# Tile 0 enters K and Q unscaled, loads are reordered, and GT runs one tile behind, in a linear-attention and SwiGLU block on one Trainium2 core

## The chip, the cores and the metric

The kernel runs on one core of one Trainium2 chip. The metric is the device time of one execution in microseconds (us), as the median of several runs. The core has five engines that run their own instruction queues and meet at semaphores: TensorE (PE in the profile; PEld is its weight load), VectorE (DVE), ScalarE (ACT), GpSimd (POOL) and SyncE (SP). SP computes nothing; here it issues most DMAs. ScalarE's queue issues some of the first ones too.

## The reference

The input x has 2048 rows of 512 numbers in bfloat16. Both branches read the same normalized rows; the result is their sum with x.

```python
def _layernorm(x, axis=-1, eps=1e-5):
    m = jnp.mean(x, axis=axis, keepdims=True)
    v = jnp.var(x, axis=axis, keepdims=True)
    return (x - m) / jnp.sqrt(v + eps)

def _A_ref(x, wqkv, wo):              # B, S, D = 1, 2048, 512
    H = 32; Dh = D // H
    q, k, v = ...                     # x @ wqkv, split into 32 heads of 16
    phi = lambda t: jnp.where(t > 0, t + 1, jnp.exp(t)) + 1e-6
    pq, pk = phi(q), phi(k)
    kv = jnp.einsum("bhsd,bhse->bhde", pk, v)
    z = jnp.einsum("bhsd->bhd", pk)
    num = jnp.einsum("bhqd,bhde->bhqe", pq, kv)
    den = jnp.einsum("bhqd,bhd->bhq", pq, z)[..., None] + 1e-6
    o = num / den
    return (...) @ wo                 # heads side by side again

def _B_ref(x, w_gate, w_up, w_down):  # F = 1792
    g = _silu(x @ w_gate)
    u = x @ w_up
    return (g * u) @ w_down

xn = _layernorm(x)
return x + _A_ref(xn, A_wqkv, A_wo) + _B_ref(xn, B_w_gate, B_w_up, B_w_down)
```

## The kernel before

The 2048 rows are 16 tiles of 128 rows. Every engine's instructions are written in an order chosen by hand: the helper class `_Prog` keeps a list for each engine and, from the keys that an operation reads and writes (`r=`, `w=`), works out the semaphore waits. It does not reorder. A DMA is entered in the list of the engine that issues it, so an engine's queue also holds up the DMAs that stand behind a wait.

The work has two phases. In the first, each tile t goes through these steps, named after the functions in the code:

- `stat(t)`: mean and variance on VectorE (`bns`, `agg`); then `rstd_pow`, which adds epsilon (L297) and raises to the power -0.5 on GpSimd (L304). For tile 0 the add is on VectorE, for the others on GpSimd.
- `xn`: (x - mean) * rstd on VectorE (L286; in halves for tile 0, L329).
- the transpose of xn into `xnT`: on TensorE with a copy by ScalarE for tiles 0 to 3 (`transpose_half`, `transpose_pe`, L313, L320), and by a DMA that SP issues for tiles 4 to 15 (`transpose_dma`, L357).
- `kproj`, `qproj`: four matmuls each into a PSUM bank, K to bank 2(t mod 2), Q to the next one (L366; for tile 0 `proj_half`, L379).
- `exp_k`, `exp_q` on ScalarE: the exponential of K and of Q, and a copy of Q (L402, L408, L412).
- `feat_k` on VectorE: clip the exponential (L419), then max(K, 0) plus it (L428). This gives phi(K), called pk.
- `zsum` on GpSimd adds up pk (L449, L453).
- `gtacc(t)`: GT, the product of xn and pk summed over all tiles in banks 4 to 7 (L461). It stands for kv: the weights of V are multiplied in afterwards.

In the loop, GT runs two tiles behind the projections: tile t's K and Q, then GT of tile t - 2. Before tile 0 is there, TensorE runs matmuls on constants (`fill`, L250) into bank 3.

The second phase is the feed-forward network, 56 steps j of one gate product and one up product (`ffn`, L567), with the finish of the attention, the down products and the output tiles put in between (L739, L750).

The first loads are issued on two queues. SP: x tile 0, x 2, the second half of K's weights, x 3, the last quarter of Q's weights, x 4, and then, after a wait for Q's weights, x 6 to 9, 10 to 11, 12 to 15. ScalarE: x 1, the first half of K's weights, half of Q's, a quarter of Q's, x 5. DMA transposes of the tiles come after all of them on SP. At t = 9 SP issues the gate and up weights in eight pieces of 448 KB each (`wpiece`, L212), then V's weights and WO; after the first z transposes, the down weights in one DMA (L209).

Of the kernel before, what the change touches and what calls it, by code (L numbers as in the profile page):

```python
# [108 lines left out]
def bass_parallel_sum__linear_attn_block__swiglu_ffn__prompt_kernel(  # L109
# [16 lines left out]
    with contextlib.ExitStack() as es:  # L126
        E = es.enter_context

        def sb(name, shape, d=bf):
            return E(nc.sbuf_tensor(name, [P] + shape, d))  # L130

        x_sb = sb("x_sb", [NT, D])
        xn_sb = sb("xn_sb", [NT, D])
        xnT = sb("xnT", [NDC, S])
        wqkv_sb = sb("wqkv_sb", [NDC, 3 * D])
        wo_sb = sb("wo_sb", [NG, D])
# [55 lines left out]
        def xload(eng, h, t0, n, after=()):  # L192
            K.dma(
                eng, lambda: h.dma_start(x_sb[:, t0:t0 + n, :], xv[:, t0:t0 + n, :]),  # L194
                r=list(after), w=[("x", t0 + i) for i in range(n)],
            )

        def wqkv_load(eng, h, name, i, c0, n):
            K.dma(
                eng,  # L200
                lambda: h.dma_start(  # L201
                    wqkv_sb[:, c0:c0 + n, i * D:(i + 1) * D],
                    A_wqkv[c0 * P:(c0 + n) * P, i * D:(i + 1) * D].rearrange("(c p) f -> p c f", p=P),
                ),
                w=[(name, c0)],
            )
# [4 lines left out]
        def wpiece(name, dst, src, c):  # L211
            K.dma("sp", lambda: sp.dma_start(dst[:, c, :], src[c * P:(c + 1) * P, :]), w=[(name, c)])  # L212
# [70 lines left out]
        def xn_dve(t):  # L283
# [52 lines left out]
        def transpose_half(t, b, h):  # L336
            tb = banks[b].bitcast(bf)[:, 0:HD].rearrange("p (c s) -> p c s", c=2)
            K.op(
                "pe",
                [  # L340
                    (lambda c=c: pe.transpose(
                        tb[:, c, :], xn_sb[:, t, (2 * h + c) * P:(2 * h + c + 1) * P], ident[:, :],
                    ))
                    for c in range(2)
                ],
                r=[("xnh", t, h), ("ident",)], w=[bk(b)],
            )
# [14 lines left out]
        def proj(t, b, lo, wname):  # L362
            K.op(
                "pe",
                [
                    (lambda c=c: pe.matmul(  # L366
                        banks[b], xnT[:, c, t * P:(t + 1) * P], wqkv_sb[:, c, lo:lo + D],
                        start=(c == 0), stop=(c == NDC - 1),
                    ))
                    for c in range(NDC)  # L370
                ],
                r=[("xnT", t), (wname, 0), (wname, 2)] + ([(wname, 3)] if wname == "wq" else []), w=[bk(b)],
            )

        def proj_half(t, b, lo, wname, h):
            K.op(
                "pe",
                [
                    (lambda c=c: pe.matmul(  # L379
                        banks[b], xnT[:, c, t * P:(t + 1) * P], wqkv_sb[:, c, lo:lo + D],  # L380
                        start=(c == 0), stop=(c == NDC - 1),
                    ))
                    for c in (2 * h, 2 * h + 1)
                ],
                r=[("xnTh", t, h), (wname, 2 * h)] + ([(wname, 3)] if wname == "wq" and h else []), w=[bk(b)],
            )

        def kb(t):
# [36 lines left out]
        def maxadd(dst, src, e, r, w):  # L425
# [54 lines left out]
        stat(0)  # L480
        stat(1)
        xn_half(0, 0)
        xn_half(0, 1)
# [6 lines left out]
        stat(4)  # L490

        fill(8, 512)
        fill(6, P, [("mv", 0)])
        fill(4, P, [("rstd", 0)])
        transpose_half(0, 4, 0)
        transpose_half(0, 5, 1)
        fill(4, P)
        proj_half(0, kb(0), D, "wk", 0)
        proj_half(0, kb(0), D, "wk", 1)
        transpose_pe(1, 6)  # L500
        exp_k(0)
        proj_half(0, qb(0), 0, "wq", 0)
        proj_half(0, qb(0), 0, "wq", 1)
        exp_q(0)
        kproj(1)
        transpose_pe(2, 7)
# [3 lines left out]
        feat_k(0)  # L510
        xn(3)
        xn(4)
        stat(5)
        kproj(2)
        transpose_pe(3, 4)
# [5 lines left out]
        stat(6)
        feat_k(2)
        gtacc(0)

        STAT = {2: (7,), 3: (8,), 4: (9, 10), 5: (11,), 6: (12,), 7: (13,), 8: (14, 15)}
        XN = {2: (6,), 3: (7,), 4: (8,), 5: (9, 10), 6: (11,), 7: (12,), 8: (13,), 9: (14, 15)}

        for t in range(2, NT):
            if t >= 3:
                kproj(t)  # L530
                exp_k(t)
                qproj(t)
                exp_q(t)
                feat_k(t)
# [4 lines left out]
            if t == 9:  # L539
                for c in range(NDC):  # L540
                    wpiece("wg", wg_sb, B_w_gate, c)
                for c in range(NDC):
                    wpiece("wu", wu_sb, B_w_up, c)
# [18 lines left out]
        def ffn_mm(j, w_sb, wname, b):  # L562
# [283 lines left out]
```

## Time and profile before

| | us |
|---|---|
| median of 3 runs (213.23 to 213.66) | 213.25 |
| the profiled execution, its own time | 213.49 |
| span of the instructions in it | 212.3 |
| DMA transposes of xn tiles: median from issue to landing, 12 of them | 2.5 |
| x, single tiles on SP: median to landing, 4 of them | 4.3 |
| gate weights, 448 KB pieces: median to landing, 4 of them | 5.5 |
| up weights, 448 KB pieces: median to landing, 4 of them | 9.0 |

The span runs from the first instruction to the last one; the run's own time also holds what lies around it. All times in a timeline are counted from the start of the span. A row of a timeline has the start, the duration, the engine, the line of the kernel, the operation, the output and its inputs, the shape, how many instructions are merged in the row, and in brackets how long the engine sat idle before and what ended that. The duration of a merged row of matmuls reaches to the end of the last one, which is still in the array when the next row starts; what a group costs the engine is read from start to start. The granted clock of TensorE was 1.00 over the whole span.

The page's row of DMA load in 40 equal slices shows when the queues are full; the second row is what was moved:

```profile
DMA  5782333897752011110101021102011010110201
GB/s 174 252 216 53 55 70 74 281 388 241 208 173 53 0 25 25 49 27 26 35 16 49 6 31 40 49 0 49 3 49 25 25 25 28 42 33 28 51 28 49
```

A slice is 5.3 us. The first three hold the loads of x and of K's and Q's weights, slices 8 to 12 the weights of the feed-forward network.

### The profile page before, as it was taken

How to read it: one execution, taken by the hardware profiler on the slowest of the kernel's cores; microseconds unless marked ns; L12 is line 12 of the kernel's file. 1: busy time of each engine (PE TensorE's matmuls, PEld its weight loads, DVE VectorE, ACT ScalarE, POOL GpSimd, SP SyncE). 2: the span in 40 equal slices, each digit the busy share in tenths (PEclk: the TensorE clock that was granted, in tenths of full speed). 3: DMA queues.
4: the chain of work that ended last, by engine and by line, in shares of the span. 5: the costliest groups of instructions: out<-in, count | busy, mean ns of one | idle time of the engine just before them, and what ended most of it. 6: DMA issues, size and time to landing. Idle time of an engine off the chain costs nothing.

```text
span 212.3 us, 2770 instructions
## 1 busy us (share of the span) xinstructions
PE 207.1 (98%) x985; PEld 96.2 (45%) x1004; DVE 119.2 (56%) x240; ACT 68.0 (32%) x118; POOL 72.7 (34%) x95
## 2 busy tenths in 40 slices
PE   7999999999999999999999999999999999999996
PEld 2444444444544444444444444444444444444454
DVE  3799997333554876546373746464656535374121
ACT  2686666666353332213122302112032213121000
POOL 2548886648021544032130442121414031221100
DMA  5782333897752011110101021102011010110201
GB/s 174 252 216 53 55 70 74 281 388 241 208 173 53 0 25 25 49 27 26 35 16 49 6 31 40 49 0 49 3 49 25 25 25 28 42 33 28 51 28 49
DMA packets 26287, 16.19 MB, mean 76 GB/s; under 512 B 18080, under 2 KB 24864, under 8 KB 26272
## 3 DMA queue, kind: packets, MB, share of 16 engines
q1 hardware_dynamic: 25296, 15.08, 25.8%
q10 hardware_dynamic: 976, 0.92, 1.4%
q8 instruction: 8, 0.13, 0.3%
q14 instruction: 7, 0.06, 0.1%
HBM read 9.70 MB, written 2.10 MB: 56 GB/s over the span
## 4 chain that ended last, share of the span: by engine, by line
PE 94%; DMA 3%; SPq 1%; issue 1%; DVE 1%
PE psum L567 45%; PE psum L750 23%; PE psum L366 12%; PE psum L739 6%; PE psum L461 6%; DMA wqkv_sb<-in_A_wqkv_dram 3%; SPq L194 1%; PE psum L665 0%; PE psum L688 0%; DVE pkq L428 0%; PE psum L379 0%; SPq L201 0%; DVE out_sb L763 0%; DVE ek L419 0%; PE psum L313 0%
## 5 line engine op out<-in xcount | busy, mean ns | idle before, releaser
L582 ACT ACTIVATE sg<-psum 128x512 bf16<-128x512 f32 x56 | 33.4, 598 | 106.9 <-PE psum L567 105.0
L567 PE MATMUL psum<-xnT,wu_sb 128*128 128x512 bf16 x222 | 57.4, 379 | 0.1
L567 PE MATMUL psum<-xnT,wg_sb 128*128 128x512 bf16 x217 | 56.0, 379 | 0.4
L697 POOL TENSOR_TENSOR prod<-pkq,zb 128x512 f32<-128x512 bf16 x16 | 18.6, 1162 | 56.0 <-DVE pkq L428 56.0
L567 PEld LDWEIGHTS psum<-xnT,wu_sb 128*128 128x128 bf16 x224 | 21.9, 98 | 26.5 <-ACT gt_sb L597 0.4
L567 PEld LDWEIGHTS psum<-xnT,wg_sb 128*128 128x128 bf16 x224 | 21.9, 98 | 26.2
L763 DVE TENSOR_TENSOR out_sb<-psum,x_sb 128x512 bf16<-128x512 f32 (+1 forms) x17 | 11.2, 660 | 36.1 <-PE psum L750 36.1
L721 POOL TENSOR_TENSOR pqn<-pkq,rden 128x512 bf16<-128x512 bf16 x16 | 16.9, 1057 | 36.6 <-DVE rden L715 36.6
L588 DVE TENSOR_TENSOR pkq<-psum,sg 128x512 bf16<-128x512 f32 x28 | 19.1, 686 | 18.2 <-PE psum L567 13.6
L366 PE MATMUL psum<-wqkv_sb,xnT 128*128 128x512 bf16 x118 | 28.4, 379 | 0.4 <-DVE pkq L428 0.3
L588 DVE TENSOR_TENSOR xn_sb<-psum,sg 128x512 bf16<-128x512 f32 x28 | 18.8, 671 | 14.2 <-PE psum L567 13.6
L750 PE MATMUL psum<-wd_sb,xn_sb 128*128 128x512 bf16 (+1 forms) x124 | 25.6, 355 | 0.1
L750 PE MATMUL psum<-wd_sb,pkq 128*128 128x512 bf16 x110 | 25.4, 379 | 0.1
L453 POOL TENSOR_TENSOR zacc<-zacc,pkq 128x512 f32<-128x512 f32 x15 | 17.3, 1156 | 7.0 <-DVE ek L419 6.8
L366 PEld LDWEIGHTS psum<-wqkv_sb,xnT 128*128 128x128 bf16 x120 | 11.6, 98 | 14.1 <-ACT xnT L320 0.6
L750 PEld LDWEIGHTS psum<-wd_sb,xn_sb 128*128 128x128 bf16 x126 | 12.3, 98 | 11.9
L750 PEld LDWEIGHTS psum<-wd_sb,pkq 128*128 128x128 bf16 x112 | 11.0, 98 | 13.2
L739 PE MATMUL psum<-m_sb,eq 128*128 128x512 bf16 (+1 forms) x66 | 16.2, 366 | 0.1
L461 PE MATMUL psum<-pkq,xn_sb 128*128 128x512 bf16 x62 | 15.8, 379 | 0.1
L705 DVE TENSOR_REDUCE den<-prod 128x32 f32<-128x512 f32 x16 | 10.9, 684 | 5.9 <-POOL prod L697 5.9
L278 DVE BATCH_NORM_STATS2 stats<-x_sb 128x6 f32<-128x512 bf16 x16 | 10.9, 683 | 4.4 <-DMA x_sb<-in_A_x_dram 4.4
L402 ACT ACTIVATE ek<-psum 128x512 bf16<-128x512 f32 x16 | 9.5, 596 | 8.9 <-DVE pkq L428 3.5
(56 smaller groups left out, 130.6 us busy)
## 6 DMA issues: line engine op xcount, KB each, us to landing
out_dram<-out_sb SPq DMA_DIRECT2D x15, 128.0 KB, 1.7
wg_sb<-in_B_w_gate_dram SPq DMA_DIRECT2D x4, 448.0 KB, 5.5
wu_sb<-in_B_w_up_dram SPq DMA_DIRECT2D x4, 448.0 KB, 9.0
wd_sb<-in_B_w_down_dram SPq DMA_DIRECT2D x1, 1792.0 KB, 7.9
x_sb<-in_A_x_dram SPq DMA_DIRECT2D x2, 512.0 KB, 4.4
x_sb<-in_A_x_dram SPq DMA_DIRECT2D x4, 128.0 KB, 4.3
wqkv_sb<-in_A_wqkv_dram ACTq DMA_DIRECT2D x2, 256.0 KB, 5.2
wqkv_sb<-in_A_wqkv_dram SPq DMA_DIRECT2D x1, 512.0 KB, 10.5
```

Source lines behind the costliest of these rows:

```text
L278: K.op("dve", lambda: dve.bn_stats(stats[:, t, :], x_sb[:, t, :]), r=[("x", t)], w=[("st", t)])
L366: (lambda c=c: pe.matmul(banks[b], xnT[:, c, t * P:(t + 1) * P], wqkv_sb[:, c, lo:lo + D], start=(c == 0), stop=(c == NDC - 1),))
L453: lambda: pool.tensor_tensor(out=zacc[:, :], in0=zacc[:, :], in1=pk, op=ALU.add),
L461: (lambda c=c: pe.matmul(banks[4 + c], xn_sb[:, t, c * P:(c + 1) * P], pkq[:, t, 0, :], start=(t == 0), stop=(t == NT - 1),))
L567: (lambda c=c: pe.matmul(banks[b], w_sb[:, c, fc * P:(fc + 1) * P], xnT[:, c, C * 512:(C + 1) * 512], start=(c == 0), stop=(c == NDC - 1),))
L582: lambda: act.activation(sg[:, j % NSG, :], banks[gb], ACT.Silu),
L588: lambda: dve.tensor_tensor(out=hT(C, fc), in0=banks[ub], in1=sg[:, j % NSG, :], op=ALU.mult,),
L697: lambda: pool.tensor_tensor(out=p, in0=pkq[:, t, 1, :], in1=zb[:, :], op=ALU.mult),
L721: lambda: pool.tensor_tensor(out=pqn[:, t % NPN, :].rearrange("p (h e) -> p h e", e=DH), in0=pkq[:, t, 1, :].rearrange("p (h e) -> p h e", ...
L739: (lambda g=g: pe.matmul(dst, pqnT(t)[:, g, :], m_sb[:, g, lo:hi], start=(g == 0), stop=False,))
L750: (lambda fc=fc: pe.matmul(dst, hT(C, fc)[:, jj * P:(jj + 1) * P], wd_sb[:, fc, lo:hi], start=False, stop=(fc == NFC - 1),))
L763: lambda: dve.tensor_tensor(out=o, in0=src, in1=x_sb[:, t, lo:hi], op=ALU.add),
```

## The change

Tile 0's x is only centred (`xc_half`: x minus mean, no rstd), transposed into a tile of its own, `xcT`, and multiplied by K's and Q's weights; ScalarE multiplies by rstd when it reads the banks (`first_ek`, `first_pk`, `first_eq`, `first_pq`). Tile 0's max(K, 0) is written to SBUF by ScalarE (`kpos`), and VectorE adds it to the clipped exponential (`first_feat`). The normalized tile 0 is still made, whole, for GT, and its `xnT` comes by a DMA transpose at t = 10.

The loads are issued in another order: SP has x 0, x 1, the second half of K's weights, the second half of Q's, x 4, then the rest of x; ScalarE has the first half of K's weights, x 2, the first half of Q's, x 3, x 5. Tile 1 is normalized and transposed in halves. Tile 3 goes to `xnT` by a DMA transpose rather than through TensorE. For tiles 1 to 4 the add of epsilon is on VectorE, and for tile 0 on GpSimd. GT runs one tile behind up to t = 10, none runs at t = 11, and from t = 12 it is two behind as before. Statistics and xn of the later tiles move back by one to two tiles. The gate and up weights are loaded in column halves (896 KB each): both first halves, V's weights, WO and the second gate half at t = 10, the second up half after the first z transposes, ahead of the down weights.

```diff
+        FH = F // 2
+        def whalf(name, dst, src, h):
...
+                    dst[:, :, h * FH:(h + 1) * FH],
+                    src[:, h * FH:(h + 1) * FH].rearrange("(c p) f -> p c f", p=P),
...
-        xload("sp", sp, 0, 1)
-        xload("act", act, 1, 1)
-        xload("sp", sp, 2, 1)
-        wqkv_load("act", act, "wk", 1, 0, 2)
-        wqkv_load("sp", sp, "wk", 1, 2, 2)
-        wqkv_load("act", act, "wq", 0, 0, 2)
-        xload("sp", sp, 3, 1)
-        wqkv_load("act", act, "wq", 0, 2, 1)
-        wqkv_load("sp", sp, "wq", 0, 3, 1)
-        xload("sp", sp, 4, 1)
-        xload("act", act, 5, 1)
-        xload("sp", sp, 6, 4, [("wq", 0), ("wq", 2), ("wq", 3)])
+        xload("sp", sp, 0, 1)
+        xload("sp", sp, 1, 1)
+        wqkv_load("act", act, "wk", 1, 0, 2)
+        wqkv_load("sp", sp, "wk", 1, 2, 2)
+        xload("act", act, 2, 1)
+        wqkv_load("act", act, "wq", 0, 0, 2)
+        wqkv_load("sp", sp, "wq", 0, 2, 2)
+        xload("act", act, 3, 1)
+        xload("sp", sp, 4, 1)
+        xload("act", act, 5, 1)
+        xload("sp", sp, 6, 4, [("wq", 0), ("wq", 2)])
         xload("sp", sp, 10, 2)
         xload("sp", sp, 12, 4)
...
+        VD = (1, 2, 3, 4)
         def rstd_pow(t):
-            eng, h = ("dve", dve) if t == 0 else ("pool", pool)
+            eng, h = ("dve", dve) if t in VD else ("pool", pool)
...
+        def xc_half(h):
...
+                    out=xc_sb[:, h * HD:(h + 1) * HD], in0=x_sb[:, 0, h * HD:(h + 1) * HD],
+                    scalar1=mv[:, 0, 0:1], scalar2=None, op0=ALU.subtract,
...
+        def first_pk():
+            K.op(
+                "act", lambda: act.activation(kpos[:, :], banks[kb(0)], ACT.Relu, scale=rstd[:, 0:1]),
+                r=[bk(kb(0)), ("rstd", 0)], w=[("kpos",)],
+            )
...
+        def first_feat():
...
+                lambda: dve.tensor_tensor(out=pkq[:, 0, 0, :], in0=kpos[:, :], in1=ek[:, 0, :], op=ALU.add),
...
         def xn(t):
             xn_dve(t)
-            if t >= 4:
+            if t >= 3:
                 transpose_dma(t)
...
+        fill(8, 512)
+        transpose_half(xc_sb, ("xc", 0), xcT, [("xcT", 0)], 4, 0)
+        fill(2, P)
+        transpose_half(xc_sb, ("xc", 1), xcT, [("xcT", 1)], 5, 1)
+        fill(10, P)
+        proj_part(xcT, ("xcT", 0), kb(0), D, "wk", 0)
+        proj_part(xcT, ("xcT", 1), kb(0), D, "wk", 1)
+        first_ek()
+        fill(3, P)
+        transpose_half(xn_sb[:, 1, :], ("xnh", 1, 0), T1, [("xnTh", 1, 0)], 6, 0)
+        transpose_half(xn_sb[:, 1, :], ("xnh", 1, 1), T1, [("xnTh", 1, 1), ("xnT", 1)], 7, 1)
+        proj_part(xcT, ("xcT", 1), qb(0), 0, "wq", 0)
+        proj_part(xcT, ("xcT", 1), qb(0), 0, "wq", 1)
+        first_pk()
+        proj_part(T1, ("xnTh", 1, 0), kb(1), D, "wk", 0)
+        proj_part(T1, ("xnTh", 1, 1), kb(1), D, "wk", 1)
+        clip(ek[:, 0, :], ("ek", 0))
...
+        first_feat()
+        transpose_pe(2, 4)
+        exp_k(1)
+        first_eq()
+        first_pq()
+        qproj(1)
+        kproj(2)
+        xn(3)
...
+        exp_q(1)
+        exp_k(2)
+        gtacc(0)
         qproj(2)
...
+        gtacc(1)
...
+        kproj(3)
...
+            if t == 10:
+                transpose_dma(0)
+                whalf("wg", wg_sb, B_w_gate, 0)
+                whalf("wu", wu_sb, B_w_up, 0)
                 wqkv_load("sp", sp, "wv", 2, 0, 4)
                 wload("sp", sp, "wo", wo_sb, A_wo)
+                whalf("wg", wg_sb, B_w_gate, 1)
...
-            if t >= 3:
+            if t >= 12:
                 gtacc(t - 2)
+            elif t < 11:
+                gtacc(t - 1)
...
         z_cols()
+        whalf("wu", wu_sb, B_w_up, 1)
         wload("sp", sp, "wd", wd_sb, B_w_down)
```

More of the change, by code (lines that the diff above doesn't have):

```diff
@@ L133, in bass_parallel_sum__linear_attn_block__swiglu_ffn__prompt_kernel @@
         xn_sb = sb("xn_sb", [NT, D])
+        xc_sb = sb("xc_sb", [D])
+        xcT = sb("xcT", [NDC, P])
+        kpos = sb("kpos", [D], f32)
         xnT = sb("xnT", [NDC, S])
@@ L196, in xload, with wqkv_load @@
             )
-        def wqkv_load(eng, h, name, i, c0, n):
+        def wqkv_load(eng, h, name, i, c0, n, after=()):
             K.dma(
@@ L204, in wqkv_load @@
                 ),
-                w=[(name, c0)],
+                r=list(after), w=[(name, c0)],
             )
@@ L209, in wload @@
             K.dma(eng, lambda: h.dma_start(dst[:, :, :], src.rearrange("(c p) f -> p c f", p=P)), w=[(name,)])
-        def wpiece(name, dst, src, c):
-            K.dma("sp", lambda: sp.dma_start(dst[:, c, :], src[c * P:(c + 1) * P, :]), w=[(name, c)])
+        FH = F // 2
+        def whalf(name, dst, src, h):
+            K.dma(
+                "sp",
+                lambda: sp.dma_start(
+                    dst[:, :, h * FH:(h + 1) * FH],
+                    src[:, h * FH:(h + 1) * FH].rearrange("(c p) f -> p c f", p=P),
+                ),
+                w=[(name, h)],
+            )
         K.op("pool", lambda: pool.memset(warm[:, :], 0.0), w=[("warm",)])
         K.op("act", lambda: act.activation(warm[:, :], warm[:, :], ACT.Exp), r=[("warm",)], w=[("warm",)])
-        xload("sp", sp, 0, 1)
-        xload("act", act, 1, 1)
-        xload("sp", sp, 2, 1)
-        wqkv_load("act", act, "wk", 1, 0, 2)
-        wqkv_load("sp", sp, "wk", 1, 2, 2)
-        wqkv_load("act", act, "wq", 0, 0, 2)
-        xload("sp", sp, 3, 1)
-        wqkv_load("act", act, "wq", 0, 2, 1)
-        wqkv_load("sp", sp, "wq", 0, 3, 1)
-        xload("sp", sp, 4, 1)
-        xload("act", act, 5, 1)
-        xload("sp", sp, 6, 4, [("wq", 0), ("wq", 2), ("wq", 3)])
-        xload("sp", sp, 10, 2)
-        xload("sp", sp, 12, 4)
         K.op("pool", lambda: pool.memset(ident[:, :], 0.0), w=[("ident",)])
@@ L241, in bass_parallel_sum__linear_attn_block__swiglu_ffn__prompt_kernel @@
         K.op("pool", lambda: pool.memset(nhalf[:, :], -0.5), w=[("nhalf",)])
+        xload("sp", sp, 0, 1)
[9 more added lines that the diff above has]
+        xload("sp", sp, 6, 4, [("wq", 0), ("wq", 2)])
+        xload("sp", sp, 10, 2)
+        xload("sp", sp, 12, 4)
         cw = nc.const_aps.tensor(1.0, (P, P), bf)
@@ L324, in bass_parallel_sum__linear_attn_block__swiglu_ffn__prompt_kernel @@
         HD = D // 2
+        def xc_half(h):
+            K.op(
+                "dve",
+                lambda: dve.tensor_scalar(
+                    out=xc_sb[:, h * HD:(h + 1) * HD], in0=x_sb[:, 0, h * HD:(h + 1) * HD],
+                    scalar1=mv[:, 0, 0:1], scalar2=None, op0=ALU.subtract,
+                ),
+                r=[("x", 0), ("mv", 0)], w=[("xc", h)],
+            )
         def xn_half(t, h):
@@ L334, in xn_half, with transpose_half @@
             )
-        def transpose_half(t, b, h):
+        def transpose_half(src, key, dst, wkeys, b, h):
             tb = banks[b].bitcast(bf)[:, 0:HD].rearrange("p (c s) -> p c s", c=2)
@@ L341, in transpose_half @@
                     (lambda c=c: pe.transpose(
-                        tb[:, c, :], xn_sb[:, t, (2 * h + c) * P:(2 * h + c + 1) * P], ident[:, :],
+                        tb[:, c, :], src[:, (2 * h + c) * P:(2 * h + c + 1) * P], ident[:, :],
                     ))
@@ L345, in transpose_half @@
                 ],
-                r=[("xnh", t, h), ("ident",)], w=[bk(b)],
+                r=[key, ("ident",)], w=[bk(b)],
             )
@@ L349, in transpose_half @@
                 "act",
-                lambda: act.activation(xnT[:, 2 * h:2 * h + 2, t * P:(t + 1) * P], tb, ACT.Copy),
-                r=[bk(b)], w=[("xnTh", t, h)] + ([("xnT", t)] if h else []),
+                lambda: act.activation(dst[:, 2 * h:2 * h + 2, :], tb, ACT.Copy),
+                r=[bk(b)], w=wkeys,
             )
@@ L371, in proj, with proj_part @@
                 ],
-                r=[("xnT", t), (wname, 0), (wname, 2)] + ([(wname, 3)] if wname == "wq" else []), w=[bk(b)],
+                r=[("xnT", t), (wname, 0), (wname, 2)], w=[bk(b)],
             )
-        def proj_half(t, b, lo, wname, h):
+        def proj_part(src, key, b, lo, wname, h):
             K.op(
@@ L379, in proj_half @@
                     (lambda c=c: pe.matmul(
-                        banks[b], xnT[:, c, t * P:(t + 1) * P], wqkv_sb[:, c, lo:lo + D],
+                        banks[b], src[:, c, :], wqkv_sb[:, c, lo:lo + D],
                         start=(c == 0), stop=(c == NDC - 1),
@@ L384, in proj_half @@
                 ],
-                r=[("xnTh", t, h), (wname, 2 * h)] + ([(wname, 3)] if wname == "wq" and h else []), w=[bk(b)],
+                r=[key, (wname, 2 * h)], w=[bk(b)],
             )
@@ L432, in maxadd, with first_ek, first_eq, first_pq @@
             )
+        def first_ek():
+            K.op(
+                "act", lambda: act.activation(ek[:, 0, :], banks[kb(0)], ACT.Exp, scale=rstd[:, 0:1]),
+                r=[bk(kb(0)), ("rstd", 0)], w=[("ek", 0)],
+            )
+        def first_pk():
+            K.op(
+                "act", lambda: act.activation(kpos[:, :], banks[kb(0)], ACT.Relu, scale=rstd[:, 0:1]),
+                r=[bk(kb(0)), ("rstd", 0)], w=[("kpos",)],
+            )
+        def first_eq():
+            K.op(
+                "act", lambda: act.activation(eq[:, 0, :], banks[qb(0)], ACT.Exp, scale=rstd[:, 0:1]),
+                r=[bk(qb(0)), ("rstd", 0)], w=[("eq", 0)],
+            )
+        def first_pq():
+            K.op(
+                "act", lambda: act.activation(pkq[:, 0, 1, :], banks[qb(0)], ACT.Identity, scale=rstd[:, 0:1]),
+                r=[bk(qb(0)), ("rstd", 0)], w=[("pq", 0)],
+            )
+        def first_feat():
+            K.op(
+                "dve",
+                lambda: dve.tensor_tensor(out=pkq[:, 0, 0, :], in0=kpos[:, :], in1=ek[:, 0, :], op=ALU.add),
+                r=[("kpos",), ("ek", 0)], w=[("pk", 0)],
+            )
         def feat_k(t):
@@ L476, in xn @@
             xn_dve(t)
-            if t >= 4:
+            if t >= 3:
                 transpose_dma(t)
[L480 to L483, printed above, removed]
+        bns(0)
+        agg(0)
+        rstd_pow(0)
+        xc_half(0)
+        xc_half(1)
+        bns(1)
+        agg(1)
+        rstd_pow(1)
+        xn_dve(0)
         bns(2)
-        xn_dve(1)
+        xn_half(1, 0)
+        xn_half(1, 1)
         agg(2)
         rstd_pow(2)
-        stat(3)
-        xn_dve(2)
@@ L490, in bass_parallel_sum__linear_attn_block__swiglu_ffn__prompt_kernel @@
[L490 to L506, printed above, removed]
-        qproj(1)
-        exp_k(1)
@@ L509, in bass_parallel_sum__linear_attn_block__swiglu_ffn__prompt_kernel @@
-        exp_q(1)
[L510 to L515, printed above, removed]
+        T1 = xnT[:, :, P:2 * P]
+        fill(8, 512)
[7 more added lines that the diff above has]
+        fill(3, P)
@@ new lines, in bass_parallel_sum__linear_attn_block__swiglu_ffn__prompt_kernel @@
+        transpose_half(xn_sb[:, 1, :], ("xnh", 1, 0), T1, [("xnTh", 1, 0)], 6, 0)
[6 more added lines that the diff above has]
+        clip(ek[:, 0, :], ("ek", 0))
+        bns(3)
+        xn_dve(2)
+        agg(3)
@@ L516, in bass_parallel_sum__linear_attn_block__swiglu_ffn__prompt_kernel @@
+        rstd_pow(3)
+        first_feat()
[3 more added lines that the diff above has]
+        first_pq()
+        qproj(1)
+        kproj(2)
+        xn(3)
+        bns(4)
+        agg(4)
+        rstd_pow(4)
+        feat_k(1)
+        bns(5)
+        xn(4)
+        agg(5)
+        rstd_pow(5)
+        exp_q(1)
+        exp_k(2)
+        gtacc(0)
         qproj(2)
-        exp_k(2)
         exp_q(2)
-        feat_k(1)
+        gtacc(1)
+        feat_k(2)
+        stat(6)
@@ L520, in bass_parallel_sum__linear_attn_block__swiglu_ffn__prompt_kernel @@
         xn(5)
[L521 to L528, printed above, removed]
-            if t >= 3:
[L530 to L534, printed above, removed]
+        kproj(3)
+        exp_k(3)
+        qproj(3)
+        exp_q(3)
@@ L535, in bass_parallel_sum__linear_attn_block__swiglu_ffn__prompt_kernel @@
+        feat_k(3)
+        stat(7)
+        xn(6)
+        gtacc(2)
+        STAT = {4: (8,), 5: (9,), 6: (10,), 7: (11, 12), 8: (13,), 9: (14, 15)}
+        XN = {4: (7,), 5: (8,), 6: (9,), 7: (10,), 8: (11, 12), 9: (13,), 10: (14, 15)}
+        for t in range(4, NT):
+            kproj(t)
+            exp_k(t)
+            qproj(t)
+            exp_q(t)
+            feat_k(t)
             for i in STAT.get(t, ()):
@@ L538, in bass_parallel_sum__linear_attn_block__swiglu_ffn__prompt_kernel @@
                 xn(i)
[L539 to L543, printed above, removed]
+            if t == 10:
+                transpose_dma(0)
+                whalf("wg", wg_sb, B_w_gate, 0)
+                whalf("wu", wu_sb, B_w_up, 0)
                 wqkv_load("sp", sp, "wv", 2, 0, 4)
                 wload("sp", sp, "wo", wo_sb, A_wo)
+                whalf("wg", wg_sb, B_w_gate, 1)
             if t == 12:
                 masks()
-            if t >= 3:
+            if t >= 12:
                 gtacc(t - 2)
+            elif t < 11:
+                gtacc(t - 1)
         zsum(NT - 2, None)
@@ L572, in ffn_mm @@
                 ],
-                r=[(wname, c) for c in range(NDC)] + [("xnT", 4 * C + i) for i in range(4)], w=[bk(b)],
+                r=[(wname, fc // (NFC // 2))] + [("xnT", 4 * C + i) for i in range(4)], w=[bk(b)],
             )
```

## The prediction

> **What bounds the kernel now.** I read the page's busy shares and its chain of waits first, then the timeline of TensorE over the first 18 us, then how long single DMAs took to land. The page:
>
> ```profile
> PE 207.1 (98%) x985; PEld 96.2 (45%) x1004; DVE 119.2 (56%) x240; ACT 68.0 (32%) x118; POOL 72.7 (34%) x95
> ...
> PE 94%; DMA 3%; SPq 1%; issue 1%; DVE 1%
> ```
>
> TensorE is the bound, and the chain that ended last is TensorE but for its first 8 us. A change of order can therefore gain only where TensorE idles, and costs wherever it makes TensorE idle. The timeline shows where that is:
>
> ```profile
> 8.42 0.59 PE L379 MATMUL psum<-wqkv_sb,xnT 128*128 128x512 bf16 x2 [0.28 <-DMA wqkv_sb<-in_A_wqkv_dram]
> ...
> 9.94 0.81 PE L366 MATMUL psum<-wqkv_sb,xnT 128*128 128x512 bf16 x3
> 11.08 1.02 PE L366 MATMUL psum<-wqkv_sb,xnT 128*128 128x512 bf16 x4 [0.33 <-DVE pkq L428]
> 11.94 0.39 PE L313 MATMUL psum<-ident,xn_sb 128*128 128x128 bf16 x4
> ...
> 13.03 1.03 PE L461 MATMUL psum<-pkq,xn_sb 128*128 128x512 bf16 x4
> 13.89 1.89 PE L366 MATMUL psum<-wqkv_sb,xnT 128*128 128x512 bf16 x8
> 15.62 1.03 PE L461 MATMUL psum<-pkq,xn_sb 128*128 128x512 bf16 x4
> 16.48 1.89 PE L366 MATMUL psum<-wqkv_sb,xnT 128*128 128x512 bf16 x8
> ```
>
> Write K0, Q0, T0, G0 for tile 0's K projection, Q projection, TensorE transpose and GT product. The rows are: second half of Q0 (8.42), after K1 and T2 Q1 (9.94), K2 (11.08), T3 (11.94), after Q2 G0 (13.03), K3 with Q3 (13.89), G1, K4. Four 512-wide matmuls take 0.863 us from start to start (13.03 to 13.89), one takes 0.216; a transpose of four pieces 0.22 (T3 11.94, Q2 12.17). From 11.08 on the engine has no gap that matters, and a tile takes 2.59 (13.89 to 16.48). So a shift of K4 carries to the end. Two waits are left: Q0's second half for Q's weights until 8.42, and K2 for VectorE to free its bank (10.80 to 11.08, 0.28).
>
> Now the SP queue. In order, each line with its issue and the time to landing: the last piece of Q's weights; the last load of x (tiles 12 to 15); the first and the second DMA transpose (tiles 4 and 5):
>
> ```profile
> L201 SPq DMA_DIRECT2D wqkv_sb<-in_A_wqkv_dram x1: 432/432/432, 2.7 to 2.7; - x1
> ...
> DMA to landing us min/median/max: 5.6/5.6/5.6
> ```
> ```profile
> L194 SPq DMA_DIRECT2D x_sb<-in_A_x_dram x1: 433/433/433, 9.2 to 9.2; - x1
> ...
> DMA to landing us min/median/max: 5.5/5.5/5.5
> ```
> ```profile
> L357 SPq DMA_TRANSPOSE xnT<-xn_sb x1: 1298/1298/1298, 11.6 to 11.6; - x1
> ...
> DMA to landing us min/median/max: 3.9/3.9/3.9
> ```
> ```profile
> L357 SPq DMA_TRANSPOSE xnT<-xn_sb x1: 1190/1190/1190, 13.8 to 13.8; - x1
> ...
> DMA to landing us min/median/max: 2.5/2.5/2.5
> ```
>
> Q's weights land at 2.70+5.6 = 8.3, and SP waits for just that before it issues x 6 to 15 (8.38, 8.75, 9.22). The last of these lands at 9.22+5.5 = 14.7. The first transpose takes 3.9, the second only 2.5: the first stood behind x 12 to 15 on SP's queue and landed at 11.61+3.9 = 15.5, just after them, and not at 11.61+2.5 = 14.1. K4 uses it at 16.48, so before this cost nothing.
>
> **The change, step by step.**
>
> *Entry by centred x.* VectorE's mean of tile 0 ends at 4.33 (aggregation, 4.15 plus 0.18). Before, two more steps (0.15 on VectorE, 0.55 on GpSimd) came before the half tiles; now these start at 4.37, and T0 on TensorE at about 4.75 instead of 5.62. The half op with one scalar is not in the trace; between 0 and the two-scalar half's 0.33 I take 0.33. Copies of 0.33 bring K0's first half to about 5.7, if its weights (first on ACT's queue now) are there. K0's second half needs the other half of K's weights, on SP behind 256 KB of x as before: issue 1.73, 4.8 to land, so 6.55. K0 ends its issue near 7.1 instead of 7.33. Then Q0's second half needs Q's other half, on SP. Ahead of it and with it go 768 KB (x 0, x 1, 256 of K, 256 of Q); before, 768 KB ended with the last Q piece too (x 0, x 2, 256 of K, x 3, 128 of Q). ACT carries 896 KB in both. I take 8.3 again, so 8.42 on TensorE. Bounds from the neighbours on the queues: 7.9 (ACT's Q piece, issued 2.35, 5.6 to land) and 9.1 (x 4, issued 3.18, 5.9 to land). The whole gain of the entry, 0.87, ends in this wait: worth 0.
>
> *What must be ready by 8.42.* VectorE: xc to 4.95, statistics of tile 1 (0.68+0.18+0.15) to 5.96, whole tile 0 (0.41) to 6.37, statistics of tile 2, whose x now stands behind K's weights on ACT (about 6.3, by K's ACT half: 1.35+5.0), to 7.05, halves of tile 1 to 7.65. T1 is on TensorE from 7.43 to 7.8, half a microsecond ahead of 8.42. GpSimd's power for tile 1 now runs beside VectorE's whole-tile xn; a GpSimd add beside that op took 0.45 (at 26.00) instead of 0.22 (at 5.42), so I add 0.23: ready at 6.83, before 7.05, no cost.
>
> The Trainium skill ("SBUF — State Buffer", Who interferes with whom) speaks against this place more strongly: a VectorE op in a two-port mode locks GpSimd out until it ends. By it the power starts only after 6.37 and ends near 7.0; the row's 0.23 is about half of such a block, and by either the sum stays.
>
> *From Q0 to G1.* From 8.42: rest of Q0 0.43, K1 0.86 (to 9.71), T2 0.22, Q1 0.86 (to 10.80). K2's bank is no longer read by VectorE, but K2 needs T2's copy on ScalarE (10.13 to 10.73, 0.15 more to TensorE): 10.88, a wait of 0.08. K2 to 11.75, G0 to 12.61. Q2 needs bank 1, which ScalarE empties in order after T2's copy, exp K1, exp Q0, copy Q0: 10.13 plus 4 x 0.60 is 12.53, 0.15 more is 12.68: a wait of 0.07. Q2 to 13.54, G1 to 14.40. The kernel before has the same work (without K3, Q3) done by 16.48 - 8 x 0.216 = 14.75. So far a gain of 0.35: T3's 0.22 and the 0.28 wait off, 0.15 of new waits on. The scaled ScalarE ops are taken as the plain ones (0.60); the added half-float, half-fp32 sum on VectorE lies between 0.26 (the clip) and 0.69 (max and add), and I take 0.69 by its fp32 input. G0 uses it two microseconds later, so both ends cost nothing.
>
> *Tile 3 goes from TensorE to a DMA transpose.* Its xn is ready near 10.8 on VectorE (x 3 lands at about 8; statistics 8.3 to 9.0; xn 2 to 9.4; the rest of the statistics, the sum and rstd to 10.4; xn 0.4). SP issues it at about 10.85, now the first transpose, and it takes the place behind x 12 to 15 that tile 4 had: landing at 15.5 however early it is issued; an issue up to 11.6 is certainly covered. K3 wants it at 14.40 and starts at 15.5+0.13 = 15.60 (0.13 as from 8.29 to 8.42). Queued behind K3 on TensorE are Q3, G2 and all the rest, and nothing else is offered to it. **This wait is 1.20.** Net: 15.60 - 14.75 = +0.85. Tile 4's transpose follows by about 16.5 and K4 wants it at 18.2.
>
> *GT one tile behind, statistics later, rstd adds on VectorE.* TensorE's count is the same. G(t-1) runs 1.73 after K(t) starts, some 4.3 after K(t-1) did; before, pk 3 was done 3.7 after K3's start (13.89; max and add 16.88 plus 0.69). VectorE still has 2.2 per 2.59 (statistics 0.68+0.18, xn 0.4, clip 0.27, max and add 0.69), and by these the DMA transposes of the later tiles land 0.7 or more before their projections. Cost 0; the cover is that 0.6 and 0.7.
>
> *Feed-forward weights.* Tile 0's DMA transpose (issue 1.2) and one more tile stand ahead on SP: issue of the first half of gate at K10 + 6.82 + 1.2 (before: K9 29.43, first gate piece 36.25), with K10 now 15.60+7x2.59 = 33.7: 41.8. Before, the first 448 KB piece landed after 3.3 and the eighth at 39.79+10.3 = 50.1, so one per 1.5. Four pieces' worth, gate and up halves, lie there at 41.8+3.3+4.5 = 49.6. The first up product ran at 50.20, just after the eighth piece (the 0.05 is gone now), and is due at 50.95. Cover 1.3. V and WO follow by 52.5 (V due 53.6); the second gate half by 55.5 and, behind the z transposes, the second up half by 63 (down's 1792 KB took 7.9, this is half), due at 64 and 64.8. Down's weights are due at 83. The z rows behind them are late by up to 2, against 0.95 on GpSimd plus 2.4 of free banks. Cost 0, gain 0.05.
>
> **Sum:** -0.35 + 1.20 - 0.05 = +0.80 on the profiled execution: span 212.3 to 213.1, its run 213.49 to 214.29. The median of the runs shown, 213.25, is 0.24 below that run; I add to the median: **214.05**. With the bounds of Q's weights (7.9 to 9.1), which move the x loads and so K3 by -0.4 to +0.8: 213.65 to 214.85.
>
> **Rivals.** (1) Tile 3 lands in time, before 14.4: then only the gain is left, -0.40, **212.85**. For it: alone a transpose takes 2.5, 10.85+2.5 = 13.35. Against it: 3.9 for the first one. (2) It lands about half way, because the loads start or run quicker: wait and gain cancel, **213.25**. (3) Slower, and elsewhere: the feed-forward halves are late. It decides once the up half lands after 50.95; pieces came 1.0 to 2.8 apart; halfway between 1.5 and 2.8 it is at 51.55: 0.6 more than my forecast, **214.65**; at 2.8 each 53.5 and 216.6.
>
> **Numbers.** Forecast 0.68, rival (1) 0.14, (2) 0.10, (3) 0.08. 0.2% is 0.43 us, about what a measurement of this kernel can tell from no change: faster 0.13 (most of rival 1), same 0.15 (rival 2, the low end of the forecast), slower 0.72. Range 212.8 to 214.9, with rival 1's value in it; the forecast's own is 213.65 to 214.85.
>
> **What will show it.** K3's first matmul after a wait of about 1.2 on a DMA, near 15.6; the first DMA transpose issued before 11.6 and landing near 15.5; TensorE's T0 at about 4.75 and yet Q0's second half at 8.4; the first gate product near 50.1 without a wait. I am wrong if K3 starts before 15, if Q0's second half starts a half microsecond away from 8.4, or if TensorE idles after 20.

## The result and the profile after

The changed kernel takes 214.25 us (median of 10 runs, 213.65 to 215.17) against 213.24 (10 runs, 212.84 to 213.97). The ratio is 1.0043, 95% interval 1.0028 to 1.0059: about 1.0 us slower.

The profiled execution of the changed kernel took 215.17 with a span of 213.9; it is the slowest of the ten, so it holds more than the median does. The page's chain of waits, shares of the span by engine:

```profile
PE 89%; DMA 4%; DVE 4%; ACT 1%; issue 0%; POOL 0%; ACTq 0%
PE psum L648 45%; PE psum L831 23%; PE psum L389 7%; PE psum L820 6%; DMA xnT<-xn_sb 4%; PE psum L515 4%; PE psum L261 2%; DVE stats L289 1%; DVE pkq L451 1%; ACT ek L425 1%; DVE ek L442 1%; PE psum L402 0%; POOL rstd L317 0%; PE psum L746 0%; PE psum L769 0%
```

Before, the DMA share was the load of Q's weights. Now it is `xnT<-xn_sb`, the DMA transpose of x tiles, 4% where it stood nowhere. The timeline of TensorE shows where:

```profile
4.32 0.40 PE L364 MATMUL psum<-ident,xc_sb 128*128 128x128 bf16 x2
...
8.37 0.60 PE L402 MATMUL psum<-wqkv_sb,xcT 128*128 128x512 bf16 x2 [0.27 <-DMA wqkv_sb<-in_A_wqkv_dram]
...
13.35 1.03 PE L515 MATMUL psum<-pkq,xn_sb 128*128 128x512 bf16 x4
15.59 1.90 PE L389 MATMUL psum<-wqkv_sb,xnT 128*128 128x512 bf16 x8 [1.22 <-DMA xnT<-xn_sb]
...
28.55 1.89 PE L389 MATMUL psum<-wqkv_sb,xnT 128*128 128x512 bf16 x8
30.28 1.03 PE L515 MATMUL psum<-pkq,xn_sb 128*128 128x512 bf16 x4
32.03 1.89 PE L389 MATMUL psum<-wqkv_sb,xnT 128*128 128x512 bf16 x8 [0.73 <-DMA xnT<-xn_sb]
```

The rows are T0's first half, the second half of Q0, G1, K3, K8, G7 and K9. There are two new waits, both on a DMA transpose of xn: before K3, and before K9. K3 was due 0.86 after G1, at 14.21, so it is 1.38 late; K9 was due 2.59 after K8, at 31.14, so it is 0.89 late (the idle shown in brackets is shorter, since a row's duration runs past the point where the next could start). Three of those DMAs, each with its issue and its time to landing, are tile 3's, tile 8's and tile 9's:

```profile
L380 SPq DMA_TRANSPOSE xnT<-xn_sb x1: 1305/1305/1305, 11.0 to 11.0; - x1
...
DMA to landing us min/median/max: 4.5/4.5/4.5
```
```profile
L380 SPq DMA_TRANSPOSE xnT<-xn_sb x1: 1189/1189/1189, 24.7 to 24.7; - x1
...
DMA to landing us min/median/max: 2.4/2.4/2.4
```
```profile
L380 SPq DMA_TRANSPOSE xnT<-xn_sb x1: 1190/1190/1190, 27.3 to 27.3; - x1
...
DMA to landing us min/median/max: 4.6/4.6/4.6
```

Tile 3's was issued at 11.0 and landed at 15.5. Tile 8's took the normal 2.4. Tile 9's took 2.2 more, and in its stretch (28.0 to 29.6 us) the list of DMA queues has two entries that are not the kernel's transfers:

```profile
q14 instruction: 1, 0.01, 5.8%
q8 instruction: 1, 0.02, 5.7%
```

The columns are packets, MB and the share of 16 engines' time in the stretch: 5.7% of 16 x 1.6 us is 1.5 us for one packet of 16 KB of instructions, and as much again for the second one, of 8 KB.

The sum over the profile: K3 at 15.59 against 14.75 for the same work before is 0.84, K9 adds 0.89, and the first feed-forward product starts at 51.02 instead of 49.29: 1.73. The two profiled runs differ by 1.68 (215.17 and 213.49).

### The profile page after: what moved, and what is told of

Read it like the earlier page. It is cut to its first block, busy times and chain, and to the rows that moved or that the text cites. A ratio compares the mean times of both kernels' runs of the same rounds, so it can differ in the third digit from the quotient of the medians.

```text
span 213.9 us, 2779 instructions
## 1 busy us (share of the span) xinstructions
PE 208.8 (98%) x1001; PEld 96.7 (45%) x1001; DVE 119.8 (56%) x245; ACT 68.2 (32%) x119; POOL 72.5 (34%) x92
## 4 chain that ended last, share of the span: by engine, by line
PE 89%; DMA 4%; DVE 4%; ACT 1%; issue 0%; POOL 0%; ACTq 0%
PE psum L648 45%; PE psum L831 23%; PE psum L389 7%; PE psum L820 6%; DMA xnT<-xn_sb 4%; PE psum L515 4%; PE psum L261 2%; DVE stats L289 1%; DVE pkq L451 1%; ACT ek L425 1%; DVE ek L442 1%; PE psum L402 0%; POOL rstd L317 0%; PE psum L746 0%; PE psum L769 0%
## 5 line engine op out<-in xcount | busy, mean ns | idle before, releaser
L648 PE MATMUL psum<-xnT,wg_sb 128*128 128x512 bf16 x224 | 57.5, 379 | 0.0
L389 PE MATMUL psum<-wqkv_sb,xnT 128*128 128x512 bf16 x116 | 27.3, 379 | 1.9 <-DMA xnT<-xn_sb 1.9
L389 PEld LDWEIGHTS psum<-wqkv_sb,xnT 128*128 128x128 bf16 x116 | 11.1, 98 | 16.0 <-DMA xnT<-xn_sb 1.7
L786 DVE TENSOR_REDUCE den<-prod 128x32 f32<-128x512 f32 x16 | 10.9, 684 | 5.7 <-POOL prod L778 5.7
L289 DVE BATCH_NORM_STATS2 stats<-x_sb 128x6 f32<-128x512 bf16 x16 | 10.9, 682 | 3.0 <-DMA x_sb<-in_A_x_dram 3.0
L425 ACT ACTIVATE ek<-psum 128x512 bf16<-128x512 f32 x15 | 9.0, 600 | 10.4 <-DVE mv L292 2.8
```

Of the source, the lines that this page charges most:

```text
L289: K.op("dve", lambda: dve.bn_stats(stats[:, t, :], x_sb[:, t, :]), r=[("x", t)], w=[("st", t)])
L389: (lambda c=c: pe.matmul(banks[b], xnT[:, c, t * P:(t + 1) * P], wqkv_sb[:, c, lo:lo + D], start=(c == 0), stop=(c == NDC - 1),))
L648: (lambda c=c: pe.matmul(banks[b], w_sb[:, c, fc * P:(fc + 1) * P], xnT[:, c, C * 512:(C + 1) * 512], start=(c == 0), stop=(c == NDC - 1),))
```

## The experiments

The changed kernel moves xn tiles by DMA transposes. The kernels below have a plain DMA of the same 128 KB in place of each one, from the same source to the same place on the same queue, in the kernel before too. Those tiles are then multiplied untransposed, so the values differ; waits, queues and matmuls stay. So they are compared with each other, and the untouched kernels above with each other. The changed kernel itself has no measurement with single edits. Every ratio is against the kernel before on the same chip, where its median was 213.24 to 213.38; the names in brackets are those of the runs.

**The base, and the change in stand-ins** (s_before, s_after).

```diff
-                lambda: sp.dma_start_transpose(out=xnT[:, :, t * P:(t + 1) * P], in_=xn_sb[:, t, :]),
+                lambda: sp.dma_start(xnT[:, :, t * P:(t + 1) * P], xn_sb[:, t, :].rearrange("p (c s) -> p c s", c=NDC)),
```

and the same for the transposes of z and of the normalized Q.

> Stand-in of the kernel before: every DMA transpose (12 of xn, 4 of z, 16 of the normalized Q) is a plain DMA of the same 128 KB from the same source to the same place on the same queue, so those tiles are multiplied untransposed and the output's values are others. All waits, queues and matmuls stay. Every theory: nothing in the kernel before waits on a transpose, so 213.2 within 0.3. It is the base for the stand-ins below.

Measured: 213.05 (212.78 to 213.72), 0.9984 of the kernel before (0.9972 to 0.9997).

> Stand-in of the changed kernel, made in the same way. Theory (the loss is tile 3's place on SP's queue behind the load of x 12 to 15, not the transpose as such): a plain copy lands after that load too, near 15, K3 starts between 15.0 and 15.6 after a wait on a DMA of 0.6 to 1.2, and the kernel is 0.3 to 0.8 slower than the stand-in of before. Rival (a DMA transpose is slow by itself, and the queue doesn't matter): the copy, issued at 11.0, lands near 13.3, K3 starts near 14.4 without a wait, and the kernel is 0.35 faster than the stand-in of before.

Measured: 213.77 (213.62 to 214.23), ratio 1.0019 (1.0007 to 1.0032): 0.72 slower than its base. The timeline of TensorE, G1 and K3:

```profile
13.21 1.03 PE L515 MATMUL psum<-pkq,xn_sb 128*128 128x512 bf16 x4
15.27 1.90 PE L389 MATMUL psum<-wqkv_sb,xnT 128*128 128x512 bf16 x8 [1.04 <-DMA xnT<-xn_sb]
```

A plain copy, issued at 10.8, lands after 4.4. So the wait before K3 does not come from transposing.

**One part of the change alone** (s_before_t3dma). Only tile 3's way is changed in the base:

```diff
-            if t >= 4:
+            if t >= 3:
                 transpose_dma(t)
...
-        transpose_pe(3, 4)
```

> One part of the change alone, on the stand-in of the kernel before: tile 3 goes by SP's queue instead of TensorE, nothing else. Theory: its copy takes the place of tile 4's behind x 12 to 15 and lands near 15.3; K3, due at 13.3 (13.54 less T3's 0.22), starts near 15.4: a wait of 2.0, net 1.8 slower than the stand-in of before (213.05), 214.85. Rival (the loss needs the change's other order, GT one behind or later statistics): within 0.3 of 213.05.

Measured: 215.24 (6 runs, 214.42 to 217.35), ratio 1.0097 (1.0060 to 1.0133): 2.2 slower than its base, by the interval 1.4 to 3.0. The timeline of TensorE, G0 and K3:

```profile
12.39 1.03 PE L461 MATMUL psum<-pkq,xn_sb 128*128 128x512 bf16 x4
14.90 1.89 PE L366 MATMUL psum<-wqkv_sb,xnT 128*128 128x512 bf16 x8 [1.48 <-issue]
```

K3, due at 13.25, is 1.65 late. The bracket names no releaser, but the copy was issued at 10.9 and took 3.9, to 14.8. The one edit makes the loss, and a larger one than the whole change, in which K3 comes a GT product later. The profiled run, 214.42, is the fastest of the six and only 1.3 above that of the base; what the others lose beyond that is not shown.

**The load of x 12 to 15 behind tile 3's copy** (s_x12).

```diff
-        xload("sp", sp, 12, 4)
...
         xn(3)
+        xload("sp", sp, 12, 4)
```

> Stand-in of the changed kernel with one edit: the load of x 12 to 15 is issued just behind tile 3's copy instead of ahead of it. Theory: the copy lands near 13.5 and K3 starts near 14.4 without a wait; 0.6 to 1.2 faster than the stand-in of the changed kernel and 0.35 faster than that of before. Rival (K3 is held by the thinner lead of the statistics, by ScalarE's queue or by the entry): K3 and the time as in the stand-in of the changed kernel.

Measured: 213.05 (212.66 to 213.28), ratio 0.9983 (0.9970 to 0.9995): 0.72 faster than s_after as forecast, but level with s_before, so the other 0.35 did not come. The timeline of TensorE, G1, K3, G2, K4:

```profile
12.92 1.03 PE L514 MATMUL psum<-pkq,xn_sb 128*128 128x512 bf16 x4
13.78 1.89 PE L388 MATMUL psum<-wqkv_sb,xnT 128*128 128x512 bf16 x8
15.51 1.03 PE L514 MATMUL psum<-pkq,xn_sb 128*128 128x512 bf16 x4
16.83 1.89 PE L388 MATMUL psum<-wqkv_sb,xnT 128*128 128x512 bf16 x8 [0.30 <-ACT pkq L434]
```

K3 follows G1 without a gap: tile 3's copy, issued at 10.9, now takes 2.4, although the load is issued at 11.7, while the copy is under way. K4, due at 16.37, is 0.46 late. The bracket names ScalarE's copy of Q3, but the wait is for several semaphores, and in s_nogate K4 starts at 16.86 while that operation still runs (16.69 to 17.28). Tile 4's copy, now the one behind the load, was issued at 13.78 and took 2.9, to 16.7: the wait moved with the place in the queue.

**The same load behind tile 4's copy** (s_x12b). In the diff above `xn(4)` stands for `xn(3)`.

> Stand-in of the changed kernel with the load of x 12 to 15 behind tile 4's copy (s_x12 had it behind tile 3's, and K4 then waited 0.4 for tile 4). Theory: no wait before K3 or K4, 0.3 to 0.5 faster than s_x12: 212.6 to 212.8, which is 0.3 to 0.4 under the stand-in of before, the gain forecast for the rest of the change. Rival (that gain is not there): 213.05.

Measured: 213.13 (212.70 to 213.77), ratio 0.9985 (0.9973 to 0.9998). Both waits are gone (K3 at 14.41 right after G1, K4 at 17.00 right after G2), yet it is no faster than s_x12 or the base. The forecast failed. Its profile shows a wait earlier on, T1 for VectorE's half tiles:

```profile
6.89 0.33 PE L260 MATMUL psum<-const-bfloat16-1.0 128*128 128x128 bf16 x3
7.77 0.54 PE L363 MATMUL psum<-ident,xn_sb 128*128 128x128 bf16 x4 [0.55 <-DVE xn_sb L351]
8.15 1.03 PE L401 MATMUL psum<-wqkv_sb,xcT 128*128 128x512 bf16 x4
```

In this execution x 1 landed at 5.4 (4.4 in s_x12), and T1 was so late that Q0 ran after it in one piece and ended at 9.01, where the base had K1 at 8.68.

**No wait for Q's weights in front of x 6 to 15** (s_nogate).

```diff
-        xload("sp", sp, 6, 4, [("wq", 0), ("wq", 2)])
+        xload("sp", sp, 6, 4)
```

> Single stand-in of the changed kernel in which SP issues the loads of x 6 to 15 at once, without the wait for Q's weights; the order of the queue is the same. Theory (tile 3's copy lands when SP's queue has moved the bytes in front of it, and the queue stands still for about 1 us between Q's weights and x 6): x 12 to 15 land about 1 earlier, tile 3's copy near 14.2, the wait before K3 falls from 1.04 to 0 to 0.4, and the kernel is 0.6 to 1.0 faster than s_after, unless Q's weights or x 5 on ScalarE's queue come later by the shared engines (then Q0's second half starts after 8.4). Rival (the late landing comes from elsewhere): as s_after, 213.77.

Measured: 213.02 (212.42 to 213.45), ratio 0.9987 (0.9972 to 1.0002): 0.75 faster than s_after by the medians, 0.7 by the ratios. The timeline of TensorE, G1 and K3:

```profile
13.41 1.03 PE L515 MATMUL psum<-pkq,xn_sb 128*128 128x512 bf16 x4
14.27 1.89 PE L389 MATMUL psum<-wqkv_sb,xnT 128*128 128x512 bf16 x8
```

K3 follows G1 without a gap. Q0's second half starts at 8.42, against 8.22 in s_after: a price of 0.2 on Q's weights, in one execution of each. Tile 3's copy is still behind all of x, but these loads are done earlier, the last at 12.2: it takes 2.4.

**Twelve more constant matmuls before K0** (s_nogate_fill22). On top of the last one:

```diff
-        fill(10, P)
+        fill(22, P)
         proj_part(xcT, ("xcT", 0), kb(0), D, "wk", 0)
```

> As s_nogate (213.02, no wait before K3), with 22 instead of 10 constant matmuls of 128 columns before K0: K0 starts 0.67 later. Theory (the earlier entry ends in the wait for Q's weights, 0.36 to 0.5 idle before Q0's second half and 0.3 to 0.4 before K0's): Q0's second half starts at 8.2 to 8.5 as before, 213.0 to 213.2. Rival (the entry is worth its time): 0.67 slower, 213.7.

Measured: 213.28 (212.49 to 213.83), ratio 0.9993 (0.9976 to 1.0010). The difference of 0.26 to s_nogate lies within the intervals, so the time alone doesn't decide. In the two profiles K0 starts at 5.94 and 5.66, so 0.28 later and not 0.67. The timeline of TensorE, K0 in halves and then Q0's first and second half, shows what the later entry met in this execution:

```profile
5.94 0.59 PE L402 MATMUL psum<-wqkv_sb,xcT 128*128 128x512 bf16 x2
6.95 0.59 PE L402 MATMUL psum<-wqkv_sb,xcT 128*128 128x512 bf16 x2 [0.41 <-DMA wqkv_sb<-in_A_wqkv_dram]
...
7.77 0.59 PE L402 MATMUL psum<-wqkv_sb,xcT 128*128 128x512 bf16 x2
8.89 0.38 PE L402 MATMUL psum<-wqkv_sb,xcT 128*128 128x512 bf16 x1 [0.53 <-DMA wqkv_sb<-in_A_wqkv_dram]
```

With twelve more constant matmuls ahead, TensorE still stands idle twice for weights. This profile has one more wait: K5 starts at 20.12, 0.43 late, after a copy of tile 5 that took 3.7.

**Tile 3 back on TensorE** (s_t3pe).

```diff
-            if t >= 3:
+            if t >= 4:
                 transpose_dma(t)
...
         xn(3)
+        transpose_pe(3, 5)
...
-        gtacc(0)
         qproj(2)
         exp_q(2)
+        gtacc(0)
```

> Stand-in of the changed kernel with tile 3's transpose back on TensorE, between K2 and Q2, and GT of tile 0 after Q2. Theory: no DMA wait before K3, but Q2 waits for ScalarE's queue until 12.5, so K3 starts near 15.1: 0 to 0.5 faster than the stand-in of the changed kernel, and slower than the one with the load moved by 0.7. Rival (the DMA route of tile 3 is no loss): slower than the stand-in of the changed kernel by T3's 0.22.

Measured: 213.42 (213.03 to 213.93), ratio 1.0003 (0.9988 to 1.0018): 0.35 faster than s_after, 0.4 slower than s_x12. Q2 waits for ScalarE's copy of Q0 as expected, but only until 11.91 (0.38 idle, `ACT pkq`) and not 12.5, and K3 starts at 14.51. As forecast it is better than the DMA behind the loads, and worse than the DMA in front of them; against s_x12 it lost less than the 0.7 expected.

**Each copy issued twice** (s2_before, s2_after, s2_xnfirst, in this order). This makes a tile's issue and landing as long as those of a DMA transpose.

```diff
         def transpose_dma(t):
+            K.dma(
+                "sp",
+                lambda: sp.dma_start(
+                    wd_sb[:, max(t - 2, 0), :].rearrange("p (c s) -> p c s", c=NDC),
+                    xn_sb[:, t, :].rearrange("p (c s) -> p c s", c=NDC),
+                ),
+                r=[("xn", t)], w=[("scr", t)],
+            )
             K.dma(
...
```

> Stand-in of the kernel before in which each xn tile's copy is issued twice, first to a place that nothing reads (in the tile of the down weights, which are loaded later), then to its own. Both issues together take 1.2 us of SP like a DMA transpose, and the second copy lands some 0.6 later than the single one, 2.4 to 2.6 after the first issue, like a transpose. Every theory: nothing waits, 213.05 within 0.2, as the single stand-in. Base for the next two.

> Stand-in of the changed kernel with each xn tile's copy issued twice in the same way. The single stand-in lost 0.72 to its base; the changed kernel lost 1.01. Theory (0.3 on average is late transposes of the tiles from 6 on: they are issued about 2.4 + 1.4 ahead of their projection, and one that an instruction fetch holds up by 1.5 to 2.2 makes TensorE wait): 0.85 to 1.1 slower than s2_before, and the profile may have a second DMA wait of up to 0.9 after 20 us. Rival (no thin lead; the 0.3 is chance): 0.72 as the single stand-in.

> As s2_after, with statistics and xn of the later tiles ahead of feat_k on VectorE's list from t = 3 on, so their copies are issued 1 us or more earlier. Theory: no DMA wait after 20 us, 0.1 to 0.4 faster than s2_after; the wait before K3 stays at 1.0 to 1.2. Rival: as s2_after.

The last has this edit, and the same at t = 3:

```diff
             exp_q(t)
-            feat_k(t)
             for i in STAT.get(t, ()):
                 stat(i)
             for i in XN.get(t, ()):
                 xn(i)
+            feat_k(t)
```

Measured: s2_before 213.12 (ratio 0.9992, 0.9977 to 1.0007), s2_after 215.08 (214.17 to 215.31, 9 runs; 1.0064, 1.0043 to 1.0086), s2_xnfirst 214.11 (213.48 to 216.39; 1.0042, 1.0018 to 1.0066). The change loses 1.96 here, twice what was expected, and the earlier statistics give half of it back (0.97, where 0.1 to 0.4 was expected; the two intervals overlap). The timeline of s2_after has both waits, K3 and K8, of which K8 was due at 28.72 (2.59 after K7):

```profile
15.76 1.90 PE L397 MATMUL psum<-wqkv_sb,xnT 128*128 128x512 bf16 x8 [1.76 <-DMA xnT<-xn_sb]
...
26.13 1.89 PE L397 MATMUL psum<-wqkv_sb,xnT 128*128 128x512 bf16 x8
27.85 1.03 PE L523 MATMUL psum<-pkq,xn_sb 128*128 128x512 bf16 x4
29.39 1.89 PE L397 MATMUL psum<-wqkv_sb,xnT 128*128 128x512 bf16 x8 [0.51 <-DMA xnT<-xn_sb]
```

Tile 8's second copy, issued at 25.4, took 3.9, and an instruction packet of 16 KB was under way after 26.0. In s2_xnfirst only the wait before K3 (1.17) is left, though a second copy issued at 19.6 took 3.3 beside such a packet. So a stretched landing makes the thin lead of the later tiles cost something; how much of it the real transposes pay is not measured by this.

**Both cures together** (s2_nogate_xnfirst), on the doubled copies:

> Doubled stand-in (as s2_after, 215.08) with both cures: the loads of x 6 to 15 issued without the wait for Q's weights, and statistics and xn ahead of feat_k. Theory: the wait before K3 (1.2 to 1.8) and the late copies after 20 us (1.0 by s2_xnfirst against s2_after) are all that is lost to s2_before: 212.8 to 213.2. Rival (a third loss): 213.5 or more.

Measured: 213.05 (212.75 to 213.30), ratio 0.9982 (0.9969 to 0.9995), level with s2_before. The only wait on a DMA left before 40 us is Q0's, at 8.39; a second copy issued at 22.1 took 4.3 beside an instruction packet, and nothing waited for it. There is no third loss, and no gain either.

## Why the prediction was right, and where it was not

- **The sum.** Forecast +0.80 to 214.05, range 212.8 to 214.9; measured 214.25. Its two main terms were each 0.2 too small, and their errors cancel: the work up to the end of G1 was done 0.54 earlier than before (14.21 against 14.75), not 0.35, and K3 then stood 1.38 late, not 1.20. This is no accident: the landing fixes K3's start, so what is gained ahead of it only lengthens the wait. The net at K3 is 0.84 against 0.85.
- **Tile 3's wait, the term that decided.** Forecast: issued at 10.85, landing at 15.5, K3 at 15.60 after 1.20. Profile: 11.00, 15.5, 15.59, 1.38. That the place in SP's queue is the cause is shown by five stand-ins: a plain copy waits as long, the edit alone brings the loss, and putting the load behind it (twice), or starting the loads earlier, takes it away. Another queue is not it: from 9 to 15.5 us the profile of the changed kernel has packets of SP's queue alone. Whether the copy stands strictly behind the load or shares the engines with it was not tested by itself; that the load issued during the copy's flight did not stretch it in s_x12 speaks for the first. The Trainium skill ("DMA: Bandwidth & Descriptors", Queues, rings and completion order) states that each DMA engine consumes a queue's descriptors in ring order; the runs agree, with 4.4 to landing behind the load and 2.4 ahead of it for the same copy.
- **The entry is worth nothing.** Forecast: T0 at 4.75 and yet Q0's second half at 8.4. Profile: 4.32 (x 0 landed at 3.0, where 3.4 was taken over from before) and 8.37, idle 0.27 for Q's weights. s_nogate_fill22 still stands for weights after a later entry.
- **Q0 to G1, the gain.** Forecast 5.98 from Q0's second half to the end of G1, against 6.33 before. Profile: 8.37 to 14.21 (13.35 and four matmuls), 5.84. The two new waits, together 0.15, did not occur. As a gain in the time, though, it is not shown: without the wait before K3 the stand-ins take 213.02 to 213.13, their bases 213.05 and 213.12, each with an interval of about 0.3 either way. The stretch is shorter: from K1 to the end of G1 it takes 5.40 to 5.54 in the nine profiles with the change's order, where the same work takes 5.71 to 5.90 in the kernel before and the two bases. But its start moves from run to run with the landing of x 1 and of the weights (Q0's second half at 7.99 to 8.89 in the profiles that have it as a row of its own). Whether the 0.35 is lost there, or is partly real, stays open.
- **"The DMA transposes of the later tiles land 0.7 or more before their projections. Cost 0".** This step failed. It leaves no room for a landing longer than usual. With the usual 2.4 tile 9 would have landed 1.4 before K9 was due, twice the cover named; it took 4.6, and K9 started 0.89 late; I had named idle after 20 us as a sign that I would be wrong. The row was there: in the kernel before, tile 7's transpose was issued at 18.83 and took 4.0, but its projection was due at 24.25. The doubled copies show the kind of loss, and that earlier statistics reduce it. Eight profiles, the changed kernel's and those of seven stand-ins, have the statistics as late as this; three of them have such a wait after 20 us: K9 here, K8 in s2_after (0.67) and K5 in s_nogate_fill22 (0.43). K9's 0.89 is as much as the profiled run lies above the median; how often the changed kernel itself has such a wait, and whether it makes up the 0.2 by which the median exceeds the forecast, was not measured.
- **GpSimd's power for tile 1.** Forecast: 0.23 longer beside VectorE's whole-tile op. Profile: it runs from 5.60 to 6.26 beside that op (5.44 to 5.84), 0.66 where most take 0.55 to 0.57: 0.1 longer, and VectorE did not idle for it. Tile 3's power was the long one: 0.92 beside `first_feat`, and VectorE idled 0.44 for it before tile 3's xn. As tile 3's landing was set by the queue, that cost nothing.
- **The feed-forward weights.** The forecast gave a first gate issue at 41.8 and a cover of 1.3. Profile: 42.74 (0.89 of it is K9's wait), the up half issued at 43.38 and landed 8.3 later, at 51.6, with the up product at 51.89. There was no stall, but the cover was 0.2: these halves took 8.9 from the first issue to the last landing where I had 7.8.

## What to carry to other kernels

A transfer that is taken off a busy engine has a place in a queue, and it is priced there: ask what stands ahead of it, and when the waiting engine wants it, not how long it takes alone (2.4) but where it stands (4.5). Order a queue by due time: here the load that was needed last stood ahead of the tile that was needed first. And keep a lead for the worst landing seen in the trace, not for the median.

## What the runs showed that was not expected

Packets of instructions stand in the profile's list of DMA queues beside the kernel's transfers, and tiles land late beside them. Each of the 14 profiles has one of 16 KB between 17 and 28 us and one of 8 KB between 24 and 30 us. The 14 have 188 DMAs of a tile into `xnT`. Of the 161 that were not issued behind a load of x under way, 29 took over 2.7 us, and each of the 29 had such a packet under way between issue and landing; 27 had one and took 2.7 or less; the 105 without one took at most 2.53. In the changed kernel all of tile 8's packets start between 25.8 and 26.7 us; about 450 of tile 9's start by 29.1, and the rest one after another until 30.5. The tile is complete only with its last packet: 4.6 instead of 2.4 in the changed kernel, 3.9 for a second copy in s2_after. The Trainium skill ("DMA: Bandwidth & Descriptors", Queues, rings and completion order) states that an engine turns to another queue only after a whole packet, which fits if the page's packet is what the profile lists as one; that the packet caused the delay is read from its place in time in all these profiles, and no run changes it.
